# A decode step on one core: weights loaded first and the FFN run early, wo in two halves, output in eight adjacent partitions with one store, filler matmuls near the end

## Chip, cores, metric

One core of one Trainium2 chip. The metric is the device time of one launch in microseconds (us), lower is better. Most executions of one kernel agree within 0.3%, but some runs fall into a slower state. Each run is labelled fast or slow, and only fast runs are compared. A ratio is the mean time of one kernel's fast runs over the mean of the other kernel's fast runs of the same rounds, so it is not quite the ratio of the medians quoted beside it.

## The reference, cut to what matters

```python
# x: [2, 1, 448]; 16 query heads, 8 KV heads, head size 256; only the last W = 2048 cache rows count
xn = layernorm(x)
q  = xn @ wq                                  # wq: [448, 4096]
p  = softmax(q . k[:, :, -2048:] * 256**-0.5) # k_cache, v_cache: [2, 8, 8192, 256]
s  = (p . v[:, :, -2048:]) @ wo               # wo: [4096, 448]
g  = silu(relu(xn @ w1) @ w2)                 # the FFN; w1: [448, 1792], w2: [1792, 448]
out = x + s * g
```

All inputs are bf16. Two sequences, one token each: every weight and every cache row is used once or twice, so the kernel mostly moves bytes.

## The kernel before

The work is cut into four units; a unit is one sequence and four KV heads. K0 to K3 and V0 to V3 are the units' 4 MB pieces of the caches. The program gives each engine its own list of operations, and waits between engines by semaphores. PE is the matrix engine, DVE and ACT are the vector and the scalar engine, and SP issues the loads. In the FFN, H is the first matmul, hT its transpose and F the second matmul.

```python
# two K buffers, two V buffers; weights borrow them while they are free
wq_sb, w1_sb, w2_sb, wo_sb = vbuf[1], kbuf[0], kbuf[0], kbuf[1]

def do_T(u, i):       # four fp32-viewed transposes of K into a PSUM bank tb, then a copy to kt[i] by DVE or ACT
def do_S(u, g):       # scores: 8 matmuls of 512 columns in four column tiles, into sbk
def softmax(u, fill): # DVE, PE, ACT in turn; PE does "fill" (P x V of the unit before) meanwhile
def do_PV(u, gs):     # P x V, 8 matmuls for each g, four column tiles
def scores(u):        # T and S of one unit, interleaved

load_k(0); load wq; load_k(1); load_v(0)
for i in range(NCHUNK): do_T(0, i)
do_q()
for g in range(4): do_S(0, g)
load_k(2); load_v(1); softmax(0)
scores(1); load_k(3); softmax(1, values(0)); attend_scale(0); load_v(2)
scores(2)
# ... load w1, w2 into kbuf[0], free since T of unit 2
softmax(2, values(1)); attend_scale(1); load_v(3, (0, 48, 64))
scores(3)
# ... load wo in five parts into kbuf[1], free since T of unit 3
softmax(3, values(2)); attend_scale(2)
do_H(); attend_turn(2); do_hT(); do_F()          # the FFN, in the shadow of V3's load
do_PV(3); attend_scale(3); attend_turn(3)
# ... two small matmuls and copies spread the attention output to at2
for j in range(32):
    deps = deps + [landed.get(j)]
    for i in range(4):                           # four column tiles: output rows 32 i and 32 i + 1
        lo = j * D + i * NCOL                    # NCOL = 112
        m_o = pr.op(PE, mm(obk[32 * i:32 * i + B, 0:NCOL], at2[:, 2 * j:2 * j + 2], wo_sb[:, lo:lo + NCOL],
                           j == 0, j == 31, tile_position=(0, 32 * i)), deps)
# ... s * g, + x on 128 partitions, then two stores (one for each sequence) from every 32nd partition
```

Of the kernel before, what the change touches and what calls it, by code (L numbers as in the profile page):

```python
# [5 lines left out]
BF = mybir.dt.bfloat16  # L6
# [70 lines left out]
def bass_recurrent_scan__sliding_block_cached__dense_activation_relu__decode_kernel(  # L77
# [28 lines left out]
    WO_PARTS = [12, 12, 4, 2, 2]  # L106
    NCOL = D // 4
    NTB = 5
# [5 lines left out]
    with es:  # L114
# [17 lines left out]
        qmask = named("qmask", [128, 4], F32)  # L132
# [3 lines left out]
        fold = named("fold", [128, 32], BF)  # L136
        fold8 = named("fold8", [128, 8], F32)
# [11 lines left out]
        h_sb = named("h_sb", [128, 28], BF)  # L149
        x_c = named("x_c", [128, NCOL], BF)  # L150
        ea = named("ea", [128, NCOL], F32)
        g_sb = named("g_sb", [128, NCOL], F32)
        tmp = named("tmp", [128, NCOL], F32)
        out_sb = named("out_sb", [128, NCOL], BF)
# [12 lines left out]
        at_exp = named("at_exp", [128, 256], BF)  # L167
        at2 = named("at2", [128, 64], BF)
# [13 lines left out]
        def kv_src(u, cache):  # L182
# [4 lines left out]
        p_xc = pr.op(POOL, lambda e: e.memset(x_c[:, :], 0.0))  # L187
        d_xc = [pr.dma(ACTE, view(x_c, 0, [[1, NCOL]], n=4, p0=b, pstep=32),
                       A_x[b, 0, :].rearrange("(i n) -> i n", i=4), [p_xc]) for b in range(B)]

        wq_sb, w1_sb, w2_sb, wo_sb = vbuf[1], kbuf[0], kbuf[0], kbuf[1]
# [4 lines left out]
        wo_src = A_wo.rearrange("(p j) n -> p (j n)", j=32)  # L196
# [7 lines left out]
        def load_v(u, cuts=(0, NT)):  # L204
            deps = [None if u == 0 else st["q_mm"] if u == 1 else st["PV", u - 2]]
            d_v[u] = []
            for lo, hi in zip(cuts, cuts[1:]):
                d_v[u].append((hi, pr.dma(SP, vbuf[u % 2][:, lo * DH:hi * DH],
                                          kv_src(u, A_v_cache)[:, :, lo * DH:hi * DH], deps)))

        load_k(0)
        d_wq = pr.dma(SP, wq_sb[:, 0:SLOTS * HC], wq_src)
        load_k(1)
        load_v(0)
# [10 lines left out]
        p_qz = pr.op(POOL, lambda e: e.memset(qz[:, :], 0.0), [p_one])  # L225

# [9 lines left out]
        for e2 in range(2):  # L236
# [10 lines left out]
            out=qmask[:, :], in_=view(ident, 0, [[32, 4], [1, 32]]), axis=AX.X, op=ALU.add))  # L247
# [4 lines left out]
        v_fold = pr.op(DVE, fold_op)  # L252
        v_f8 = pr.op(DVE, lambda e: e.tensor_reduce(
# [103 lines left out]

        def do_PV(u, gs=range(4)):
            bank, src, p = obk, vbuf[u % 2], pt[u % 2]
            for g in gs:  # L360
                deps = [next(d for hi, d in d_v[u] if hi >= 16 * g + 16), st["pt", u], a_z, st["obk"]]
                for a in range(2):
                    for i in range(4):
                        lo = (16 * g + 4 * i + 2 * a) * DH
                        o = pr.op(PE, mm(bank[32 * i:32 * i + 16, :],
                                         p[:, 256 * a + 64 * i + 16 * g:256 * a + 64 * i + 16 * g + 16], src[:, lo:lo + 2 * DH],
                                         g == 0 and a == 0, g == 3 and a == 1, tile_position=(0, 32 * i)), deps)
                        deps = []
            st["PV", u] = o

        def attend_scale(u):
            st["osb", u] = st["obk"] = pr.op(DVE, lambda e: e.tensor_scalar(  # L372
                out=o_sb[:, :], in0=obk[:, :], scalar1=rs[:, u:u + 1], scalar2=None, op0=ALU.mult),
                [st["PV", u], st["rs", u], st.get(("oT", u - 1))])

        def attend_turn(u):
            b, v = divmod(u, 2)
            deps = [st["osb", u], v_fold, st["mbk"]]
            for dhi in range(2):
                for tp in range(2):  # L380
                    o = pr.op(PE, mm(mbk_ap(136 + 8 * dhi, 8), o_sb[:, 256 * tp + 128 * dhi:256 * tp + 128 * dhi + 128],
                                     fold[:, 8 * tp:8 * tp + 8], tp == 0, tp == 1), deps)
                    deps = []
            st["oT", u] = o
            st["at", u] = st["mbk"] = pr.op(DVE, lambda e: e.tensor_tensor(
                out=view(at_exp, 128 * b + 64 * v, [[8, 8], [4, 2], [1, 4]]),
                in0=view(mbk, 136, [[1, 8], [8, 2], [0, 4]]),
                in1=view(qmask, 0, [[0, 8], [0, 2], [1, 4]]), op=ALU.mult), [o, v_qm])
# [35 lines left out]
        def do_hT():  # L424
            hbk = tb[0][:, :].bitcast(F32).tensor
            deps = [st["h_n"], evac[NU * NCHUNK - 4]]
            for j in range(7):
                for i in range(4):
                    o = pr.op(PE, mm(view(hbk, 4 * j, [[1, 4]], n=32, p0=32 * i), view(h_n, j, [[7, 32]]),
                                     ident[:, 32 * i:32 * i + 4], j == 0, tile_position=(0, 32 * i)), deps)  # L430
                    deps = []
            st["hT"] = pr.op(DVE, lambda e: e.tensor_copy(
                view(h_sb, 0, [[2, 7], [14, 2], [1, 2]]), view(hbk, 0, [[4, 7], [2, 2], [1, 2]])), [o])

        def do_F():
            fbk = tb[1][:, :].bitcast(F32).tensor
            deps = [st["w2"], st["hT"], evac[NU * NCHUNK - 3]]
            for f in range(14):
                for i in range(4):
                    lo = W2_AT + f * D + i * NCOL  # L440
                    o = pr.op(PE, mm(view(fbk, 0, [[1, NCOL]], n=B, p0=32 * i), h_sb[:, 2 * f:2 * f + 2], w2_sb[:, lo:lo + NCOL],
                                     f == 0, f == 13, tile_position=(0, 32 * i)), deps)
                    deps = []
            f_ap = view(fbk, 0, [[1, NCOL]])
            a_e = pr.op(ACTE, lambda e: e.activation(ea[:, :], f_ap, ACT.Exp, scale=-1.0), [o])
            v_d = pr.op(DVE, lambda e: e.tensor_scalar(
                out=ea[:, :], in0=ea[:, :], scalar1=1.0, scalar2=None, op0=ALU.add), [a_e])
            v_rc = pr.op(DVE, lambda e: e.reciprocal(tmp[:, :], ea[:, :]), [v_d])
            st["g"] = pr.op(DVE, lambda e: e.tensor_tensor(
                out=g_sb[:, :], in0=f_ap, in1=tmp[:, :], op=ALU.mult), [v_rc])  # L450

        def scores(u):
            for i in range(NCHUNK):
# [3 lines left out]
                if i == 3 and u > 1:  # L457
                    attend_turn(u - 2)
            do_S(u, 3)
# [4 lines left out]
        for i in range(NCHUNK):  # L464
            do_T(0, i)
        do_q()
        for g in range(4):
            do_S(0, g)
# [9 lines left out]
        st["w1"] = pr.dma(SP, w1_sb[:, 0:W2_AT], w1_src, [st["T", 2]])  # L478
        st["w2"] = pr.dma(SP, w2_sb[:, W2_AT:W2_AT + 14 * D].rearrange("p (hf f) -> p hf f", hf=2), w2_src,
                          [st["T", 2]])  # L480
        softmax(2, values(1))
        attend_scale(1)
        load_v(3, (0, 48, 64))
        scores(3)
        d_wo = []
        j0 = 0
        for n in WO_PARTS:
            d_wo.append((j0, pr.dma(SP, wo_sb[:, j0 * D:(j0 + n) * D], wo_src[:, j0 * D:(j0 + n) * D], [st["T", 3]])))
            j0 += n
        softmax(3, values(2))  # L490
        attend_scale(2)
        do_H()
        attend_turn(2)
        do_hT()
        do_F()
        do_PV(3)
        attend_scale(3)
        attend_turn(3)
        for b in range(2):
            m_at = pr.op(PE, mm(mbk_ap(256 + 32 * b, 32), at_exp[:, 128 * b:128 * b + 128],  # L500
                                fold[:, :], True, True), [st["at", NU - 1], v_fold, st["mbk"]])
            v_at2 = st["mbk"] = pr.op(DVE, lambda e, b=b: e.tensor_copy(
                view(at2, b, [[2, 32]]), mbk_ap(256 + 32 * b, 32)), [m_at])
        deps = [v_at2, st["obk"]]
        landed = dict(d_wo)
        for j in range(32):
            deps = deps + [landed.get(j)]
            for i in range(4):
                lo = j * D + i * NCOL
                m_o = pr.op(PE, mm(obk[32 * i:32 * i + B, 0:NCOL], at2[:, 2 * j:2 * j + 2], wo_sb[:, lo:lo + NCOL],  # L510
                                   j == 0, j == 31, tile_position=(0, 32 * i)), deps)
                deps = []
        v_t = pr.op(DVE, lambda e: e.tensor_tensor(
            out=tmp[:, :], in0=obk[:, 0:NCOL], in1=g_sb[:, :], op=ALU.mult), [m_o, st["g"]])
        v_o = pr.op(DVE, lambda e: e.tensor_tensor(
            out=out_sb[:, :], in0=tmp[:, :], in1=x_c[:, :], op=ALU.add), [v_t, *d_xc])
        d_o = [pr.dma((SP, ACTE)[b], out[b, 0, :].rearrange("(i n) -> i n", i=4),
                      view(out_sb, 0, [[1, NCOL]], n=4, p0=b, pstep=32), [v_o]) for b in range(B)]
        pr.op(SP, None, d_o)
# [31 lines left out]
```

## Time and profile before

| | before |
|---|---|
| time, median of the first 3 runs | 112.66 us (112.59 to 112.87) |
| span of the profiled run, first to last instruction | 110.9 us |
| bytes moved by the load queue | 44.11 MB, busy 93.5% of the span |
| K0 landed / K3 landed | 13.1 / 71.6 us |
| last softmax begins (reduction of scores of unit 3) | 82.62 us |
| wo's matmuls begin / end | 102.38 / 107.9 us |

The transfer table on the profile page of the kernel before gives, for each queue, packets, MB and the share of 16 engines' span:

```profile
q1 hardware_dynamic: 2584, 44.11, 93.5%
```

Its windows view, cut to the steady part, has the columns: start:end and length in us, busy time of each engine with its instruction count, mean granted clock of PE (1.00 is full), mean busy share of the DMA engines, GB/s:

```profile
4.00:104.00 100.00, 71.58 (x765) 48.19 (x765) 46.52 (x105) 33.85 (x42) 0.00 (x0) 0.87 1.00 429
```

For 100 us the DMA engines have a busy share of 1.00 at 429 GB/s. PE is at 71.58 us of 100.

The chain of waits of the kernel before (start, length, what), its ends alone:

```profile
0.74 12.35 DMA kbuf<-in_A_k_cache_dram
...
46.36 25.27 DMA kbuf<-in_A_k_cache_dram
...
83.07 24.39 DMA kbuf<-in_A_wo_dram
107.46 0.04 issue
107.50 0.39 PE obk L265 x8
107.89 0.02 issue
107.91 0.28 DVE tmp L513
108.19 0.02 issue
108.22 0.27 DVE out_sb L515
```

It ends in wo's last piece, and after it only 8 matmuls, two vector operations and the store are left.

The view of who waited for whom (engine, line, what it waited for: us in total, times, longest) has PE waiting for three kinds of loads only:

```profile
PE tb L285 <- DMA kbuf<-in_A_k_cache_dram: 6.3, 2, 5.4
...
PE obk L265 <- DMA vbuf<-in_A_v_cache_dram: 3.5, 1, 3.5
...
PE obk L265 <- DMA kbuf<-in_A_wo_dram: 1.8, 2, 1.6
```

Of the 6.3 us, 5.4 are the wait for K0 and 0.9 the wait for K3. So from 13.13 us to 70.8 us PE never waits for a transfer: it works, or it waits for DVE and ACT, in the softmax above all. The last softmax begins here (timeline of the kernel before):

```profile
82.62 0.69 DVE L318 TENSOR_REDUCE rm<-sbk 128x4 f32<-128x512 f32 x1 [0.73 <-PE sbk L265]
```

PE's slack is 0.9 us at K3 and whatever lies after the last softmax: the FFN, which has time there, and 3.5 us of waiting for V3. The timeline of the tail (start, length, engine, line, operation, tensors, count, idle time before and its cause) shows this, and shows that wo's matmuls come in bursts as its parts land:

```profile
96.35 3.59 PE L265 MATMUL obk<-vbuf,pt 128*16 128x512 bf16 x32 [3.49 <-DMA vbuf<-in_A_v_cache_dram]
...
102.38 1.29 PE L265 MATMUL obk<-kbuf,at 128*2 128x112 bf16 x48 [0.29 <-DVE at L502]
...
105.29 2.01 PE L265 MATMUL obk<-kbuf,at 128*2 128x112 bf16 x72 [1.62 <-DMA kbuf<-in_A_wo_dram]
...
107.50 0.36 PE L265 MATMUL obk<-kbuf,at 128*2 128x112 bf16 x8 [0.20 <-DMA kbuf<-in_A_wo_dram]
```

### The profile page before, as it was taken

The numbers are of one execution on the slowest core, as the hardware profiler recorded it, in microseconds if no ns is written. First come the engines' busy times: TensorE is split into PE (matmuls) and PEld (weight loads), VectorE is DVE, ScalarE is ACT, GpSimd is POOL, SyncE is SP. The second block draws the span as 40 slices with busy tenths as digits, with TensorE's granted clock in tenths as the row PEclk, the third lists the DMA queues.
The fourth block names the chain that finished last, engine by engine and source line by source line (L and its number), as shares of the span: only waits on it lengthen the run. The fifth ranks groups of instructions, "written<-read, shape, count | busy, mean of one in ns | idle before, by whom it ended". The sixth has DMA issues, their size and how long they took to land.

```text
span 110.9 us, 1921 instructions
## 1 busy us (share of the span) xinstructions
PE 74.0 (67%) x845; PEld 49.7 (45%) x845; DVE 48.0 (43%) x110; ACT 35.4 (32%) x43; POOL 1.9 (2%) x11
## 2 busy tenths in 40 slices
PE   0010299995428999859999949699985464293480
PEld 0000299952127977413777513397632244022350
DVE  2182042953433356553775653477546333104001
ACT  1960036760020647602286602076820200000000
POOL 6000000000000000000000000000000000000000
PEclk9999999999995589995899995799999985555555
DMA  3988979898899889889989998998999999999920
GB/s 95 473 379 379 520 331 496 355 567 372 378 532 414 378 378 556 384 378 532 417 366 390 526 402 378 520 426 378 387 382 416 454 434 423 408 426 427 394 98 1
DMA packets 2619, 44.22 MB, mean 399 GB/s; under 512 B 306, under 2 KB 564, under 8 KB 948
## 3 DMA queue, kind: packets, MB, share of 16 engines
q1 hardware_dynamic: 2584, 44.11, 93.5%
q8 instruction: 6, 0.10, 0.3%
q10 hardware_dynamic: 28, 0.00, 0.0%
q14 instruction: 1, 0.01, 0.0%
HBM read 44.11 MB, written 0.00 MB: 398 GB/s over the span
## 4 chain that ended last, share of the span: by engine, by line
DMA 56%; PE 34%; DVE 4%; SPq 2%; issue 1%; ACT 1%
DMA kbuf<-in_A_k_cache_dram 34%; PE tb L285 25%; DMA kbuf<-in_A_wo_dram 22%; PE sbk L265 5%; PE obk L265 2%; SPq L36 2%; PE mbk L265 1%; DVE s_sb L335 1%; ACT e_sb L340 1%; DVE rm L318 1%; DVE q_n L399 1%; PE mbk L345 1%; DVE pt L350 0%; DVE qz L409 0%; PE mbk L403 0%
## 5 line engine op out<-in xcount | busy, mean ns | idle before, releaser
L285 PE MATMUL tb<-ident_f,kbuf 128*128 128x128 f32 x256 | 36.6, 306 | 6.3 <-DMA kbuf<-in_A_k_cache_dram 6.3
L285 PEld LDWEIGHTS tb<-ident_f,kbuf 128*128 128x128 f32 x256 | 33.5, 161 | 10.4 <-DMA kbuf<-in_A_k_cache_dram 6.4
L295 ACT ACTIVATE kt<-tb 128x1024 bf16<-128x1024 bf16 x28 | 27.4, 1023 | 26.2 <-PE tb L285 26.2
L293 DVE COPY kt<-tb 128x1024 bf16<-128x1024 bf16 x36 | 24.7, 690 | 21.7 <-PE tb L285 21.7
L265 PE MATMUL obk<-vbuf,pt 128*16 128x512 bf16 x128 | 13.5, 529 | 3.5 <-DMA vbuf<-in_A_v_cache_dram 3.5
L265 PE MATMUL sbk<-kt,qz 128*32 128x512 bf16 x128 | 11.0, 393 | 1.7 <-DVE kt L293 1.1
L340 ACT ACTIVATE e_sb<-s_sb 128x512 bf16<-128x512 f32 x4 | 2.5, 630 | 22.9 <-DVE s_sb L335 22.9
L265 PEld LDWEIGHTS obk<-vbuf,pt 128*16 128x16 bf16 x128 | 3.2, 101 | 8.2 <-DMA vbuf<-in_A_v_cache_dram 4.4
L265 PE MATMUL mbk<-ident,xg 2*128 2x2 bf16 x7 | 0.3, 163 | 7.4 <-DVE xg L237 7.4
L372 DVE TENSOR_SCALAR o_sb<-obk,rs 128x512 bf16<-128x512 f32 x4 | 2.9, 735 | 5.4 <-PE obk L265 5.4
L265 PEld LDWEIGHTS sbk<-kt,qz 128*32 128x32 bf16 x128 | 2.7, 94 | 5.5 <-DVE kt L293 2.1
L265 PE MATMUL obk<-kbuf,at 128*2 128x112 bf16 x128 | 3.7, 292 | 2.1 <-DMA kbuf<-in_A_wo_dram 1.8
L318 DVE TENSOR_REDUCE rm<-sbk 128x4 f32<-128x512 f32 x4 | 2.8, 691 | 4.3 <-PE sbk L265 4.3
L350 DVE COPY pt<-mbk 128x512 bf16<-128x512 bf16 x4 | 1.7, 424 | 5.6 <-PE mbk L345 5.6
L345 PE MATMUL mbk<-ident,e_sb 128*128 128x128 bf16 x16 | 2.2, 286 | 2.6 <-ACT e_sb L340 2.6
L265 PEld LDWEIGHTS obk<-kbuf,at 128*2 128x2 bf16 x128 | 2.6, 112 | 3.1 <-DMA kbuf<-in_A_wo_dram 2.6
L265 PEld LDWEIGHTS mbk<-ident,xg 2*128 2x128 bf16 x7 | 0.3, 101 | 7.4 <-DVE xg L237 7.4
L345 PEld LDWEIGHTS mbk<-ident,e_sb 128*128 128x128 bf16 x16 | 1.3, 122 | 5.0 <-ACT e_sb L340 5.0
L323 PE MATMUL mbk<-ident_f,rm 128*1 128x128 f32 x4 | 1.1, 270 | 3.4 <-DVE rm L321 3.4
L265 PE MATMUL mbk<-one_f,mall 1*128 1x1 f32 x8 | 1.6, 268 | 2.5 <-DVE mall L330 2.5
L335 DVE SCALAR_TENSOR_TENSOR s_sb<-sbk,bias,low 128x512 f32<-128x512 f32 x4 | 3.0, 751 | 0.1
L323 PEld LDWEIGHTS mbk<-ident_f,rm 128*1 128x1 f32 x4 | 0.3, 79 | 5.4 <-DVE rm L321 5.4
(68 smaller groups left out, 37.0 us busy)
## 6 DMA issues: line engine op xcount, KB each, us to landing
kbuf<-in_A_k_cache_dram SPq DMA_DIRECT2D x4, 4096.0 KB, 27.1
vbuf<-in_A_v_cache_dram SPq DMA_DIRECT2D x3, 4096.0 KB, 37.0
vbuf<-in_A_wq_dram SPq DMA_DIRECT2D x1, 3584.0 KB, 20.1
kbuf<-in_B_w_dram SPq DMA_DIRECT2D x2, 1568.0 KB, 23.6
vbuf<-in_A_v_cache_dram SPq DMA_DIRECT2D x1, 3072.0 KB, 25.8
kbuf<-in_A_wo_dram SPq DMA_DIRECT2D x2, 1344.0 KB, 22.2
vbuf<-in_A_v_cache_dram SPq DMA_DIRECT2D x1, 1024.0 KB, 27.7
kbuf<-in_A_wo_dram SPq DMA_DIRECT2D x1, 448.0 KB, 24.3
```

What stands on the lines that cost most here:

```text
L36: o = _Op(eng, lambda e: e.dma_start(dst, src), [d for d in deps if d is not None], True)
L265: return lambda e: e.matmul(out_ap, lhsT=lhsT, rhs=rhs, start=start, stop=stop, skip_group_check=True, **kw)
L285: o = pr.op(PE, lambda e, n=n, lo=lo: e.matmul(bank_f[:, n * 128:(n + 1) * 128], lhsT=src_f[:, lo:lo + 128], rhs=ident_f[:, :], start=True ...
L293: evac[n_th] = pr.op(DVE, lambda e: e.tensor_copy(dst[:, :], bank[:, :]), deps)
L295: evac[n_th] = pr.op(ACTE, lambda e: e.activation(dst[:, :], bank[:, :], ACT.Copy), deps)
L318: v = pr.op(DVE, lambda e: e.tensor_reduce(out=rm4[:, :], in_=view(sbk, 0, [[1, 4], [4, 128]]), axis=AX.X, op=ALU.max), [st["S", u]])
L323: m = st["rmT", u] = pr.op(PE, lambda e: e.matmul(mbk_ap(0, 128, 1), lhsT=rm[:, :], rhs=ident_f[:, :], start=True, stop=True, is_transpose ...
L335: v = st["shift", u] = pr.op(DVE, lambda e: e.scalar_tensor_tensor(out=view(s_sb, 0, [[4, 128], [1, 4]]), in0=view(sbk, 0, [[4, 128], [1, ...
L340: a = st["exp", u] = pr.op(ACTE, lambda e: e.activation(e_sb[:, :], s_sb[:, :], ACT.Exp, accum_out=ssum[:, 0:1]), [v, st.get(("Pt", u - 1) ...
L345: o = pr.op(PE, lambda e, j=j: e.matmul(mb16[:, 512 + 128 * j:640 + 128 * j], lhsT=e_sb[:, 128 * j:128 * j + 128], rhs=ident[:, :], start= ...
L350: v = st["pt", u] = pr.op(DVE, lambda e: e.tensor_copy(view(pt[u % 2], 0, [[256, 2], [16, 16], [8, 2], [1, 8]]), view(mb16, 512, [[256, 2] ...
L372: st["osb", u] = st["obk"] = pr.op(DVE, lambda e: e.tensor_scalar(out=o_sb[:, :], in0=obk[:, :], scalar1=rs[:, u:u + 1], scalar2=None, op0 ...
```

## The change

The intent: get the small weights and the whole FFN out of the way at the start, so that the end has less to do; let half of wo's work depend on half of the heads; shorten the end with a compact output and one store; and keep PE busy near the end so that its clock stays up.

The core of the diff (cut):

```diff
-        wq_sb, w1_sb, w2_sb, wo_sb = vbuf[1], kbuf[0], kbuf[0], kbuf[1]
+        wq_sb, w1_sb, w2_sb, wo_sb = vbuf[1], vbuf[0], vbuf[0], kbuf[0]
...
-            deps = [None if u == 0 else st["q_mm"] if u == 1 else st["PV", u - 2]]     # load_v
+            deps = [st["F"] if u == 0 else st["q_mm"] if u == 1 else st["PV", u - 2]]
...
+        d_wq = pr.dma(SP, wq_sb[:, 0:SLOTS * HC], wq_src)
+        st["w1"] = pr.dma(SP, w1_sb[:, 0:W2_AT], w1_src)
+        st["w2"] = pr.dma(SP, w2_sb[:, ...], w2_src)
         load_k(0)
-        d_wq = pr.dma(SP, wq_sb[:, 0:SLOTS * HC], wq_src)
         load_k(1)
-        load_v(0)
...
-        for i in range(NCHUNK):
-            do_T(0, i)
         do_q()
-        for g in range(4):
-            do_S(0, g)
+        do_H()
+        do_hT()
+        do_F()
+        load_v(0)
+        scores(0)
...
         attend_scale(2)
-        do_H()
-        attend_turn(2)
-        do_hT()
-        do_F()
-        do_PV(3)
+        idle_work(3)                  # 3 matmuls of 512 columns that nobody reads
+        do_PV(3, (0,))                # P x V of unit 3, now into another bank (tb[3])
+        attend_turn(2)
+        do_PV(3, (1,))
+        attend_spread(2)
+        do_PV(3, (2, 3))
         attend_scale(3)
+        idle_work(3)
         attend_turn(3)
-        for b in range(2): ...        # two spreads, one after the other
+        idle_work(1)
+        attend_spread(3)
...
-                m_o = pr.op(PE, mm(obk[32 * i:32 * i + B, 0:NCOL], at2[:, 2 * j:2 * j + 2], wo_sb[:, lo:lo + NCOL],
-                                   j == 0, j == 31, tile_position=(0, 32 * i)), deps)
+                m_o = pr.op(PE, mm(obk[0:NROW, 0:NCOL], at_z[:, j * GAP + 3 - i:j * GAP + 3 - i + NROW],
+                                   wo_sb[:, lo:lo + NCOL], j == 0 and i == 0, j == 2 * NWO - 1 and i == 3), deps)
...
-        d_o = [pr.dma((SP, ACTE)[b], ...) for b in range(B)]
+        d_o = pr.dma(ACTE, out[:, 0, :].rearrange("b (i n) -> (b i) n", i=4), out_sb[:, :], [v_o])
```

In the new layout each of the four 112-column pieces writes all eight output rows; the weights are zero except in the two columns that belong to its own piece, and a shift of the window into a zero-padded buffer selects them. The FFN's second matmul (F) has the same layout. wo's parts became 6, 6, 4, 4, 4, 4, 2, 2 slices instead of 12, 12, 4, 2, 2, and its buffer is free already after the transposes of unit 2.

More of the change, by code (lines that the diff above doesn't have):

```diff
@@ L105, in bass_recurrent_scan__sliding_block_cached__dense_activation_relu__decode_kernel @@
     FC = DFF // 2
-    WO_PARTS = [12, 12, 4, 2, 2]
+    WO_PARTS = [6, 6, 4, 4, 4, 4, 2, 2]
+    NWO = 16
     NCOL = D // 4
+    NROW = 4 * B
+    GAP = NROW + 3
     NTB = 5
@@ L131, in bass_recurrent_scan__sliding_block_cached__dense_activation_relu__decode_kernel @@
         par2 = named("par2", [128, 2], F32)
-        qmask = named("qmask", [128, 4], F32)
+        qmask = named("qmask", [128, 8], F32)
         own = named("own", [128, 4], F32)
@@ L136, in bass_recurrent_scan__sliding_block_cached__dense_activation_relu__decode_kernel @@
         fold = named("fold", [128, 32], BF)
+        fold16 = named("fold16", [128, NWO], BF)
         fold8 = named("fold8", [128, 8], F32)
@@ L148, in bass_recurrent_scan__sliding_block_cached__dense_activation_relu__decode_kernel @@
         h_n = named("h_n", [128, FC // 4], BF)
-        h_sb = named("h_sb", [128, 28], BF)
-        x_c = named("x_c", [128, NCOL], BF)
-        ea = named("ea", [128, NCOL], F32)
-        g_sb = named("g_sb", [128, NCOL], F32)
-        tmp = named("tmp", [128, NCOL], F32)
-        out_sb = named("out_sb", [128, NCOL], BF)
+        h_z = named("h_z", [128, 14 * GAP], BF)
+        x_c = named("x_c", [NROW, NCOL], BF)
+        ea = named("ea", [NROW, NCOL], F32)
+        g_sb = named("g_sb", [NROW, NCOL], F32)
+        tmp = named("tmp", [NROW, NCOL], F32)
+        out_sb = named("out_sb", [NROW, NCOL], BF)
         rm4 = named("rm4", [128, 4], F32)
@@ L166, in bass_recurrent_scan__sliding_block_cached__dense_activation_relu__decode_kernel @@
         o_sb = named("o_sb", [128, 512], BF)
-        at_exp = named("at_exp", [128, 256], BF)
-        at2 = named("at2", [128, 64], BF)
+        at_exp = named("at_exp", [128, 128], BF)
+        at_z = named("at_z", [128, 32 * GAP], BF)
         kbuf = [named(f"kbuf{i}", [128, UW], BF) for i in range(2)]
@@ L186, in bass_recurrent_scan__sliding_block_cached__dense_activation_relu__decode_kernel @@
         d_x = pr.dma(ACTE, x_sb[0:B, :], A_x[:, 0, :])
-        p_xc = pr.op(POOL, lambda e: e.memset(x_c[:, :], 0.0))
-        d_xc = [pr.dma(ACTE, view(x_c, 0, [[1, NCOL]], n=4, p0=b, pstep=32),
-                       A_x[b, 0, :].rearrange("(i n) -> i n", i=4), [p_xc]) for b in range(B)]
-        wq_sb, w1_sb, w2_sb, wo_sb = vbuf[1], kbuf[0], kbuf[0], kbuf[1]
+        d_xc = pr.dma(ACTE, x_c[:, :], A_x[:, 0, :].rearrange("b (i n) -> (b i) n", i=4))
+        wq_sb, w1_sb, w2_sb, wo_sb = vbuf[1], vbuf[0], vbuf[0], kbuf[0]
         W2_AT = SLOTS * FC
@@ L195, in bass_recurrent_scan__sliding_block_cached__dense_activation_relu__decode_kernel @@
         w2_src = B_w2.rearrange("(hf p j) n -> p hf (j n)", hf=2, j=7)
-        wo_src = A_wo.rearrange("(p j) n -> p (j n)", j=32)
+        wo_src = A_wo.rearrange("(v p j) n -> v p (j n)", v=2, j=NWO)
         assert SLOTS * HC <= UW and 32 * D <= UW and W2_AT + 14 * D <= UW
@@ L209, in load_v @@
                                           kv_src(u, A_v_cache)[:, :, lo * DH:hi * DH], deps)))
+        d_wq = pr.dma(SP, wq_sb[:, 0:SLOTS * HC], wq_src)
+        st["w1"] = pr.dma(SP, w1_sb[:, 0:W2_AT], w1_src)
+        st["w2"] = pr.dma(SP, w2_sb[:, W2_AT:W2_AT + 14 * D].rearrange("p (hf f) -> p hf f", hf=2), w2_src)
         load_k(0)
-        d_wq = pr.dma(SP, wq_sb[:, 0:SLOTS * HC], wq_src)
         load_k(1)
-        load_v(0)
         i0 = pr.op(POOL, lambda e: e.memset(ident[:, :], 0.0))
@@ L225, in bass_recurrent_scan__sliding_block_cached__dense_activation_relu__decode_kernel @@
         p_qz = pr.op(POOL, lambda e: e.memset(qz[:, :], 0.0), [p_one])
+        p_z = [pr.op(POOL, lambda e, t=t: e.memset(t[:, :], 0.0)) for t in (h_z, at_z)][-1]
         a_z = [pr.op(ACTE, lambda e, t=t: e.memzero(t[:, :])) for t in (obk,)][-1]
@@ L246, in bass_recurrent_scan__sliding_block_cached__dense_activation_relu__decode_kernel @@
         v_qm = pr.op(DVE, lambda e: e.tensor_reduce(
-            out=qmask[:, :], in_=view(ident, 0, [[32, 4], [1, 32]]), axis=AX.X, op=ALU.add))
+            out=qmask[:, :], in_=view(ident, 0, [[16, 8], [1, 16]]), axis=AX.X, op=ALU.add))
         def fold_op(e):
@@ L252, in bass_recurrent_scan__sliding_block_cached__dense_activation_relu__decode_kernel, with fold16_op @@
         v_fold = pr.op(DVE, fold_op)
+        def fold16_op(e):
+            with nc.allow_low_precision("zeros and ones"):
+                return e.tensor_reduce(out=fold16[:, :], in_=view(ident, 0, [[1, NWO], [NWO, 8]]), axis=AX.X, op=ALU.add)
+        v_fold16 = pr.op(DVE, fold16_op)
         v_f8 = pr.op(DVE, lambda e: e.tensor_reduce(
@@ L356, in softmax, with out_bank @@
             assert not fill
+        obk_last = tb[3][:, :].bitcast(F32).tensor
+        def out_bank(u):
+            return obk if u < NU - 1 else obk_last
         def do_PV(u, gs=range(4)):
-            bank, src, p = obk, vbuf[u % 2], pt[u % 2]
+            bank, src, p = out_bank(u), vbuf[u % 2], pt[u % 2]
             for g in gs:
-                deps = [next(d for hi, d in d_v[u] if hi >= 16 * g + 16), st["pt", u], a_z, st["obk"]]
+                deps = [next(d for hi, d in d_v[u] if hi >= 16 * g + 16), st["pt", u], a_z if u < NU - 1 else st["tb3"], st["obk"]]
                 for a in range(2):
@@ L371, in attend_scale @@
         def attend_scale(u):
-            st["osb", u] = st["obk"] = pr.op(DVE, lambda e: e.tensor_scalar(
-                out=o_sb[:, :], in0=obk[:, :], scalar1=rs[:, u:u + 1], scalar2=None, op0=ALU.mult),
+            v = st["osb", u] = pr.op(DVE, lambda e: e.tensor_scalar(
+                out=o_sb[:, :], in0=view(out_bank(u), 0, [[1, 512]]), scalar1=rs[:, u:u + 1], scalar2=None, op0=ALU.mult),
                 [st["PV", u], st["rs", u], st.get(("oT", u - 1))])
+            if u < NU - 1:
+                st["obk"] = v
         def attend_turn(u):
-            b, v = divmod(u, 2)
             deps = [st["osb", u], v_fold, st["mbk"]]
@@ L385, in attend_turn, with attend_spread @@
             st["at", u] = st["mbk"] = pr.op(DVE, lambda e: e.tensor_tensor(
-                out=view(at_exp, 128 * b + 64 * v, [[8, 8], [4, 2], [1, 4]]),
-                in0=view(mbk, 136, [[1, 8], [8, 2], [0, 4]]),
-                in1=view(qmask, 0, [[0, 8], [0, 2], [1, 4]]), op=ALU.mult), [o, v_qm])
+                out=view(at_exp, 0, [[16, 8], [8, 2], [1, 8]]),
+                in0=view(mbk, 136, [[1, 8], [8, 2], [0, 8]]),
+                in1=view(qmask, 0, [[0, 8], [0, 2], [1, 8]]), op=ALU.mult), [o, v_qm, st.get(("m_at", u - 1))])
+        def attend_spread(u):
+            b, v = divmod(u, 2)
+            o = st["m_at", u] = pr.op(PE, mm(mbk_ap(256, NWO), at_exp[:, :], fold16[:, :], True, True),
+                                      [st["at", u], v_fold16, st["mbk"]])
+            st["at_z", v] = st["mbk"] = pr.op(DVE, lambda e: e.tensor_copy(
+                view(at_z, NWO * GAP * v + 3 + 4 * b, [[GAP, NWO]]), mbk_ap(256, NWO)), [o, p_z])
         def do_q():
@@ L425, in do_hT @@
             hbk = tb[0][:, :].bitcast(F32).tensor
-            deps = [st["h_n"], evac[NU * NCHUNK - 4]]
+            deps = [st["h_n"]]
             for j in range(7):
@@ L431, in do_hT @@
                     deps = []
-            st["hT"] = pr.op(DVE, lambda e: e.tensor_copy(
-                view(h_sb, 0, [[2, 7], [14, 2], [1, 2]]), view(hbk, 0, [[4, 7], [2, 2], [1, 2]])), [o])
+            st["hT"] = evac[-NTB] = pr.op(DVE, lambda e: e.tensor_copy(
+                view(h_z, 3, [[GAP, 7], [7 * GAP, 2], [4, 2]]), view(hbk, 0, [[4, 7], [2, 2], [1, 2]])), [o, p_z])
         def do_F():
             fbk = tb[1][:, :].bitcast(F32).tensor
-            deps = [st["w2"], st["hT"], evac[NU * NCHUNK - 3]]
+            deps = [st["w2"], st["hT"]]
             for f in range(14):
@@ L440, in do_F @@
                     lo = W2_AT + f * D + i * NCOL
-                    o = pr.op(PE, mm(view(fbk, 0, [[1, NCOL]], n=B, p0=32 * i), h_sb[:, 2 * f:2 * f + 2], w2_sb[:, lo:lo + NCOL],
-                                     f == 0, f == 13, tile_position=(0, 32 * i)), deps)
+                    o = pr.op(PE, mm(view(fbk, 0, [[1, NCOL]], n=NROW), h_z[:, f * GAP + 3 - i:f * GAP + 3 - i + NROW],
+                                     w2_sb[:, lo:lo + NCOL], f == 0 and i == 0, f == 13 and i == 3), deps)
                     deps = []
-            f_ap = view(fbk, 0, [[1, NCOL]])
+            st["F"] = o
+            f_ap = view(fbk, 0, [[1, NCOL]], n=NROW)
             a_e = pr.op(ACTE, lambda e: e.activation(ea[:, :], f_ap, ACT.Exp, scale=-1.0), [o])
@@ L448, in do_F, with idle_work @@
             v_rc = pr.op(DVE, lambda e: e.reciprocal(tmp[:, :], ea[:, :]), [v_d])
-            st["g"] = pr.op(DVE, lambda e: e.tensor_tensor(
+            st["g"] = evac[1 - NTB] = pr.op(DVE, lambda e: e.tensor_tensor(
                 out=g_sb[:, :], in0=f_ap, in1=tmp[:, :], op=ALU.mult), [v_rc])
+        def idle_work(n):
+            wbk = tb[2][:, :].bitcast(F32).tensor
+            deps = [evac[NU * NCHUNK - 2], v_fold]
+            for _ in range(n):
+                pr.op(PE, mm(view(wbk, 0, [[1, 512]]), ident[:, :], kt[0][:, 0:512], True, True), deps)
+                deps = []
         def scores(u):
@@ L458, in scores @@
                     attend_turn(u - 2)
+                if i == 5 and u > 1:
+                    attend_spread(u - 2)
             do_S(u, 3)
@@ L477, in bass_recurrent_scan__sliding_block_cached__dense_activation_relu__decode_kernel @@
         scores(2)
-        st["w1"] = pr.dma(SP, w1_sb[:, 0:W2_AT], w1_src, [st["T", 2]])
-        st["w2"] = pr.dma(SP, w2_sb[:, W2_AT:W2_AT + 14 * D].rearrange("p (hf f) -> p hf f", hf=2), w2_src,
-                          [st["T", 2]])
         softmax(2, values(1))
@@ L483, in bass_recurrent_scan__sliding_block_cached__dense_activation_relu__decode_kernel @@
         load_v(3, (0, 48, 64))
-        scores(3)
-        d_wo = []
-        j0 = 0
-        for n in WO_PARTS:
-            d_wo.append((j0, pr.dma(SP, wo_sb[:, j0 * D:(j0 + n) * D], wo_src[:, j0 * D:(j0 + n) * D], [st["T", 3]])))
-            j0 += n
+        d_wo, j0 = {}, 0
+        for n in WO_PARTS:
+            v, j = divmod(j0, NWO)
+            d_wo[j0] = pr.dma(SP, wo_sb[:, j0 * D:(j0 + n) * D], wo_src[v, :, j * D:(j + n) * D], [st["T", 2]])
+            j0 += n
+        scores(3)
+        st["tb3"] = pr.op(ACTE, lambda e: e.memzero(tb[3][:, :]), [evac[NU * NCHUNK - 1]])
@@ L490, in bass_recurrent_scan__sliding_block_cached__dense_activation_relu__decode_kernel @@
         softmax(3, values(2))
         attend_scale(2)
-        do_H()
+        idle_work(3)
+        do_PV(3, (0,))
         attend_turn(2)
-        do_hT()
-        do_F()
-        do_PV(3)
+        do_PV(3, (1,))
+        attend_spread(2)
+        do_PV(3, (2, 3))
         attend_scale(3)
+        idle_work(3)
         attend_turn(3)
-        for b in range(2):
-            m_at = pr.op(PE, mm(mbk_ap(256 + 32 * b, 32), at_exp[:, 128 * b:128 * b + 128],
-                                fold[:, :], True, True), [st["at", NU - 1], v_fold, st["mbk"]])
-            v_at2 = st["mbk"] = pr.op(DVE, lambda e, b=b: e.tensor_copy(
-                view(at2, b, [[2, 32]]), mbk_ap(256 + 32 * b, 32)), [m_at])
@@ L504, in bass_recurrent_scan__sliding_block_cached__dense_activation_relu__decode_kernel @@
-        deps = [v_at2, st["obk"]]
-        landed = dict(d_wo)
-        for j in range(32):
-            deps = deps + [landed.get(j)]
+        idle_work(1)
+        attend_spread(3)
+        deps = [st["obk"]]
+        for j in range(2 * NWO):
+            deps = deps + [d_wo.get(j), st["at_z", j // NWO]]
             for i in range(4):
                 lo = j * D + i * NCOL
-                m_o = pr.op(PE, mm(obk[32 * i:32 * i + B, 0:NCOL], at2[:, 2 * j:2 * j + 2], wo_sb[:, lo:lo + NCOL],
-                                   j == 0, j == 31, tile_position=(0, 32 * i)), deps)
+                m_o = pr.op(PE, mm(obk[0:NROW, 0:NCOL], at_z[:, j * GAP + 3 - i:j * GAP + 3 - i + NROW],
+                                   wo_sb[:, lo:lo + NCOL], j == 0 and i == 0, j == 2 * NWO - 1 and i == 3), deps)
@@ L512, in bass_recurrent_scan__sliding_block_cached__dense_activation_relu__decode_kernel @@
                 deps = []
         v_t = pr.op(DVE, lambda e: e.tensor_tensor(
-            out=tmp[:, :], in0=obk[:, 0:NCOL], in1=g_sb[:, :], op=ALU.mult), [m_o, st["g"]])
+            out=tmp[:, :], in0=obk[0:NROW, 0:NCOL], in1=g_sb[:, :], op=ALU.mult), [m_o, st["g"]])
         v_o = pr.op(DVE, lambda e: e.tensor_tensor(
-            out=out_sb[:, :], in0=tmp[:, :], in1=x_c[:, :], op=ALU.add), [v_t, *d_xc])
-        d_o = [pr.dma((SP, ACTE)[b], out[b, 0, :].rearrange("(i n) -> i n", i=4),
-                      view(out_sb, 0, [[1, NCOL]], n=4, p0=b, pstep=32), [v_o]) for b in range(B)]
@@ L519, in bass_recurrent_scan__sliding_block_cached__dense_activation_relu__decode_kernel @@
-        pr.op(SP, None, d_o)
+            out=out_sb[:, :], in0=tmp[:, :], in1=x_c[:, :], op=ALU.add), [v_t, d_xc])
+        d_o = pr.dma(ACTE, out[:, 0, :].rearrange("b (i n) -> (b i) n", i=4), out_sb[:, :], [v_o])
+        pr.op(ACTE, None, [d_o])
         with nc.Block() as block:
```

## The prediction

> **What bounds it now.** The page's transfer table: 44.11 MB, SP's queue busy 93.5% of the 110.9 us span. Windows show about 427 GB/s from 2.4 us on, with no gap, and the chain of waits ends in wo's last piece (landed 107.46), then 8 matmuls (0.39), two vector operations (0.6) and the store (2.4). Bytes do not change; the tail leaves at most about 1 us to win.
>
> **PE is nearly as tight.** The timeline shows no DMA wait on PE between K0's landing (13.13) and 70.8 us, where K3 comes 0.9 us late. The slack is in the last stage: H, hT and F (89.1 to 92.9) and a 3.5 us wait for V3 before 96.35.
>
> **What the change moves.** Landings of before fit 3.15 us + cumulative bytes / 0.4215 MB per us (K0 13.1, wq 21.5, K3 71.6, end 107.5). With wq, w1, w2 ahead, K0 lands at about 29.4 instead of 13.1. Moved out of its path: q (3.4 us) and H/hT/F, which were free in the slack. From there the serial work per unit, from the timeline (scores to score maximum, then softmax to the next transpose): 13.2+5.9, 13.2+6.1, 10.8+6.1, 10.9+5.5 = 71.7 us. The two 13.2 include a slow clock at their start (28 transposes in 5.68 us; at full clock 16 take 1.90). So softmax 3 ends near 101 us (before: 88.1), after V3 has landed (about 99). I see no new DMA starvation: V0 waits for F (about 25 us, queue full to 39), K2, V1, K3, V2, V3 are all issued before the queue drains. wo still lands near 107.5, but no longer matters.
>
> **Tail after 101.** Fillers, PV3 with turn and spread of unit 2 (about 3 us), scale 0.75, turn, spread (about 1.2): wo's matmuls start near 106 (before: 102.4). Before, four column tiles ran together: 56 such matmuls of 112 columns took 1.47 us at half clock, 26 ns each. Now the eight adjacent rows put all in one column group, so they run one after another: 4 x 26 = about 105 ns cold, about 50 warm (bf16 transposes of 128 columns step about 50 ns at full clock: four in 0.40 us). The Trainium skill ("TensorE: Matmul & The Clock Gate", Part 3 and "Back-to-back issue gap") agrees: tiles overlap by column group; alone N/2.4+2.5 ns, and 81 ns for load/matmul pairs at N=128. 128 of them: estimate 6.4 us warm, 10 at the pair rate, 13 cold; I take 7. End of wo about 113, plus 3.0 us for combine and store: span 116, timed 117.8.
>
> Single store, no memset, 8-partition vector work: under 0.3 us together. Smaller wo pieces: nothing. Fillers: about 1.5 us of PE, partly hidden behind the scale; they hold the clock up for wo.
>
> **Prediction: 117.8 us, range 114.9 to 121.5. Faster 2%, same 13%, slower 85%.**
>
> **Right if** the profile shows K0's landing near 29 us; PE waiting for no transfer after that; softmax 3 ending near 101; wo's matmuls one stream of 6 to 10 us starting near 106, with all wo landed before they finish; the chain of waits running through PE and DVE from K0 to the end instead of ending in a wo transfer.
>
> **Wrong if** the clock is granted earlier than before in the first two score stages (up to 2.4 us each) and wo runs warm: then the wo transfer bounds again and the time is about 112.5. Or worse, if weight loads are exposed or the clock stays at 0.5 in the tail: 121 and more. Or if transfers starve somewhere in the middle.

## The result, and the profile after

| | before | after |
|---|---|---|
| time, median | 112.71 us (112.59 to 112.87, 4 runs) | 119.18 us (117.83 to 120.74, 4 runs) |
| fast runs | all 4 | 117.91 and 117.83 |
| ratio of fast runs | | 1.0457, 95% interval 1.0432 to 1.0482 |
| span of the profiled run | 110.9 us | 116.1 us (fast) |
| K0 landed | 13.1 us | 30.25 us |
| last softmax begins | 82.62 us | 96.19 us |
| wo's matmuls begin / end | 102.38 / 107.9 us | 107.4 / 113.9 us |

The change is slower by 4.6%. Two of its four runs fell at 120.5 and 120.7 us, which is why its median lies so far above the fast runs; the fast runs alone are used below.

The transfers hardly got slower. The transfer table on the profile page of the kernel after:

```profile
q1 hardware_dynamic: 3008, 44.11, 90.0%
```

Its windows view over the same stretch as before:

```profile
4.00:104.00 100.00, 74.19 (x690) 49.17 (x692) 45.77 (x104) 33.56 (x42) 0.00 (x0) 0.86 1.00 424
```

The busy share is 1.00 again, at 424 GB/s, and of the page's 40 slices each from the second to the 36th has the DMA engines at 80% or more: no stretch is starved. The chain of waits of the kernel after, however, is another one:

```profile
2.11 28.14 DMA kbuf<-in_A_k_cache_dram
30.25 0.04 issue
30.29 5.00 PE tb L294 x28
...
107.48 6.40 PE obk L274 x128
...
113.91 0.27 DVE tmp L542
...
114.20 0.26 DVE out_sb L544
```

The first reduction of the last softmax (timeline of the kernel after) comes 13.6 us later than before:

```profile
96.19 0.69 DVE L327 TENSOR_REDUCE rm<-sbk 128x4 f32<-128x512 f32 x1 [0.73 <-PE sbk L274]
```

After K0's landing at 30.25 us no DMA stands in the chain any more; from there to the end it runs through PE, DVE and ACT, and its last large piece is one unbroken stretch of 128 matmuls. In the view of who waited for whom, for the kernel after, PE's waits for loads are now all in the first 31 us:

```profile
PE tb L294 <- DMA kbuf<-in_A_k_cache_dram: 5.8, 1, 5.8
...
PE obk L274 <- DMA vbuf<-in_A_wq_dram: 5.2, 1, 5.2
...
PE tb L274 <- DMA vbuf<-in_B_w_dram: 0.6, 1, 0.6
```

PE waits for loads only until K0 has landed; after that no load holds it up. The tail in the timeline of the kernel after, beside that of before:

```profile
102.45 0.59 PE L274 MATMUL tb<-kt,ident 128*128 128x512 bf16 x2
...
102.49 0.73 DVE L386 TENSOR_SCALAR o_sb<-obk,rs 128x512 bf16<-128x512 f32 x1
...
103.37 0.61 PE L274 MATMUL tb<-vbuf,pt 128*16 128x512 bf16 x8 [0.33 <-DVE o_sb L386]
...
105.72 0.82 PE L274 MATMUL tb<-kt,ident 128*128 128x512 bf16 x3
105.85 0.75 DVE L386 TENSOR_SCALAR o_sb<-tb,rs 128x512 bf16<-128x512 f32 x1 [0.75 <-PE tb L274]
...
106.66 0.26 PE L274 MATMUL mbk<-fold,o_sb 128*128 128x8 bf16 x4
...
107.41 6.46 PE L274 MATMUL obk<-kbuf,at_z 128*8 128x112 bf16 x128
```

The last line is wo: the 128 matmuls that before came in bursts, at 27 to 28 ns each (2.01 us for 72, granted clock 0.50), with waits for transfers between them, now take 6.40 us in one piece, 50 ns each, and wait for nothing. The windows view of the kernel after, cut to this stretch, shows that its clock is full and that the transfers are over:

```profile
107.40:114.00 6.60, 6.47 (x129) 6.29 (x128) 0.32 (x2) 0.00 (x0) 0.00 (x0) 1.00 0.01 3
```

The fillers (the lines `tb<-kt,ident`) run while DVE does its two scale operations. The first line shows two of the three: a few matmul records are missing from a trace. The first P x V of unit 3 still waits 0.33 us for the first scale operation after the fillers before it are done.

### The profile page after: what moved, and what is told of

Read it like the earlier page. It is cut to its first block, busy times and chain, and to the rows that moved or that the text cites. A ratio compares the mean times of both kernels' runs of the same rounds, so it can differ in the third digit from the quotient of the medians.

```text
span 116.1 us, 1945 instructions
## 1 busy us (share of the span) xinstructions
PE 83.8 (72%) x853; PEld 56.5 (49%) x854; DVE 49.0 (42%) x113; ACT 35.9 (31%) x44; POOL 2.3 (2%) x12
## 4 chain that ended last, share of the span: by engine, by line
PE 56%; DMA 24%; DVE 13%; ACT 2%; issue 2%; SPq 1%
PE tb L294 30%; DMA kbuf<-in_A_k_cache_dram 24%; PE obk L274 10%; PE sbk L274 8%; PE mbk L274 4%; DVE kt L302 2%; DVE rm L327 2%; PE mbk L354 2%; DVE s_sb L344 2%; ACT e_sb L349 2%; PE tb L274 2%; DVE o_sb L386 1%; SPq L36 1%; DVE mrow L335 1%; PE mbk L332 1%
## 5 line engine op out<-in xcount | busy, mean ns | idle before, releaser
L294 PEld LDWEIGHTS tb<-ident_f,kbuf 128*128 128x128 f32 x256 | 32.4, 158 | 11.3 <-DMA kbuf<-in_A_k_cache_dram 6.0
L302 DVE COPY kt<-tb 128x1024 bf16<-128x1024 bf16 x36 | 24.8, 691 | 21.6 <-PE tb L294 21.1
L274 PE MATMUL sbk<-kt,qz 128*32 128x512 bf16 x128 | 12.0, 394 | 1.5 <-DVE kt L302 1.5
L274 PE MATMUL obk<-vbuf,pt 128*16 128x512 bf16 x96 | 11.0, 550 | 0.0
L274 PE MATMUL obk<-vbuf,xr 128*4 128x512 bf16 (+1 forms) x56 | 4.6, 506 | 5.2 <-DMA vbuf<-in_A_wq_dram 5.2
L274 PE MATMUL obk<-kbuf,at_z 128*8 128x112 bf16 x128 | 6.5, 213 | 0.0
L274 PEld LDWEIGHTS obk<-kbuf,at_z 128*8 128x8 bf16 x128 | 6.3, 87 | 0.0
L274 PE MATMUL tb<-vbuf,h_z 128*8 128x112 bf16 x56 | 4.7, 275 | 0.6 <-DMA vbuf<-in_B_w_dram 0.6
L274 PEld LDWEIGHTS obk<-vbuf,xr 128*4 128x4 bf16 x56 | 1.6, 115 | 7.2 <-DMA vbuf<-in_A_wq_dram 5.3
L274 PEld LDWEIGHTS tb<-vbuf,h_z 128*8 128x8 bf16 x56 | 4.6, 118 | 0.7 <-DMA vbuf<-in_B_w_dram 0.7
L274 PEld LDWEIGHTS obk<-vbuf,pt 128*16 128x16 bf16 x96 | 2.4, 100 | 2.8 <-issue 1.9
```

The costliest lines, as they stand in the source:

```text
L274: return lambda e: e.matmul(out_ap, lhsT=lhsT, rhs=rhs, start=start, stop=stop, skip_group_check=True, **kw)
L294: o = pr.op(PE, lambda e, n=n, lo=lo: e.matmul(bank_f[:, n * 128:(n + 1) * 128], lhsT=src_f[:, lo:lo + 128], rhs=ident_f[:, :], start=True ...
L302: evac[n_th] = pr.op(DVE, lambda e: e.tensor_copy(dst[:, :], bank[:, :]), deps)
```

## Experiments

Two causes were in the prediction: K0 lands late, so that PE's serial work moves past the end of the transfers (theory A), and wo's matmuls lost their packing (theory B). Rivals: one of the two alone is the whole loss; the fillers are on the path; or the transfers are starved. The last is already answered by the busy share above. All eight kernels gave correct results.

### e1_order_only: the load order and the early FFN alone

```diff
 # on the kernel before
+        load wq; load w1; load w2            # w1, w2 into vbuf[0]; V0 waits for F
         load_k(0)
-        load wq
         load_k(1)
-        load_v(0)
...
-        T(0); q; S(0)
+        do_q(); do_H(); do_hT(); do_F(); load_v(0); scores(0)
...                                            # wo into kbuf[0], after T of unit 2
-        do_H(); attend_turn(2); do_hT(); do_F(); do_PV(3)
+        attend_turn(2); do_PV(3)
```

> Before, with only the new load order (wq, w1, w2, K0, K1, V0 after F), FFN first, and wo behind V3 in the buffer that K2 frees; four column tiles, layouts and store as before. My theory (K0 late makes the PE chain of about 72 us the bound): K0 lands near 30, softmax 3 ends near 102, wo's matmuls start at 107 to 109 and take 2 to 3.5 us as four tiles: 115.0 to 117.0 us, no PE wait for a wo transfer. Rival (the serial wo stream is what costs, the order alone is harmless): 112 to 113.5 us. Second rival (the whole loss is the order, the layout costs nothing): 117.5 to 118.5.

Measured: 115.28 us median (114.17 to 117.37, 4 runs, one of them slow); ratio 1.0183 (1.0128 to 1.0237). The verdict at 2% is "unclear", but the interval excludes no loss. In the timeline of e1:

```profile
96.77 0.69 DVE L319 TENSOR_REDUCE rm<-sbk 128x4 f32<-128x512 f32 x1 [0.73 <-PE sbk L266]
...
108.36 2.11 PE L266 MATMUL obk<-kbuf,at 128*2 128x112 bf16 x128 [0.29 <-DVE at L499]
```

The last softmax begins at 96.77 us, as late as in the kernel after, and wo's 128 matmuls wait for no part of wo. So the order alone moves the bound to PE, and costs about 2 us (fast runs 114.91 us on average, against 112.85 for before). Part of the 2.11 us is a falling clock: windows of e1 show it at 1.00 up to 109.2 us and at 0.50 from 109.6 us, 0.79 on average over the stream. It is not the whole loss, and it is not harmless: two of the three expectations are excluded.

### e2_wo_tiled: the eight-row layout alone undone

```diff
 # on the kernel after (F likewise; combine on 128 rows and two stores as before)
-   mm(obk[0:NROW, 0:NCOL], at_z[:, j * GAP + 3 - i:j * GAP + 3 - i + NROW], wo_sb[...], ...)
+   mm(obk[32 * i:32 * i + B, 0:NCOL], view(at_z, j * GAP + 3, [[4, B]]), wo_sb[...], ..., tile_position=(0, 32 * i))
```

> After, with only the eight adjacent rows undone: FFN's second and wo's matmuls again in four column tiles, 128-row combine, two stores. My theory: wo takes 2 to 3.4 us where it took 6.4, the store 0.8 more: 114.5 to 116 us in the faster state, still slower than before by 2 to 3%, since K0 still lands near 30. Rival (the serial stream is the whole loss): about 112.7. Rival (packing does not matter here, the stream is bound by something else): 118 to 119.

Measured: 114.29 us (114.0 to 116.73, 4 runs, one slow); ratio to before 1.0127 (1.0103 to 1.0151). wo's matmuls in the timeline of e2:

```profile
107.35 1.75 PE L276 MATMUL obk<-kbuf,at_z 128*2 128x112 bf16 x128
```

The windows view of e2, cut to that stretch:

```profile
107.40:109.20 1.80, 1.69 (x129) 1.52 (x128) 0.28 (x2) 0.00 (x0) 0.00 (x0) 1.00 0.04 13
```

The stream starts at the same time as in the kernel after (107.35 against 107.41 us) at the same full clock, and takes 1.70 us by the chain of waits instead of 6.40: 13 ns a matmul instead of 50. I had expected 2 to 3.4 us. The 3.4 is 128 times the 26 ns that the kernel before showed at half clock; halved for the full clock that is 1.7, and my lower end of 2 did not go that far. Four tiles at full clock ran here at about a quarter of the serial time. Of the 4.7 us won the strided stores take back about 0.8 (below), and the ratio of the two ratios, 1.0457 / 1.0127, is 3.3% or 3.7 us. The remainder, 1.3% or 1.4 us, is what the new order costs here, with the two halves and the fillers still in place; in e1, without them, it cost 2.1. The packing alone is not the whole loss either.

### e3_no_fill: the kernel after without the fillers

```diff
-        idle_work(3)    # before P x V of unit 3
-        idle_work(3)    # during the scale of unit 3
-        idle_work(1)    # before the spread of unit 3
```

> After, without the seven filler matmuls. My theory: they sit in PE's waits for the two scale operations, so taking them away saves at most 0.3 us by itself; the clock may drop in the tail, and then the serial wo stream starts at half clock (50 ns becomes 95 ns each until it is granted again): 117.8 to 121. Rival (the fillers are a cost on the path): 116.5 to 117.2.

Measured: 118.46 us (117.86 to 120.54, 4 runs, one slow); ratio 1.0479 (1.0440 to 1.0519), not to be told from the 1.0457 of the kernel after. wo's matmuls in the timeline of e3:

```profile
108.22 6.46 PE L274 MATMUL obk<-kbuf,at_z 128*8 128x112 bf16 x128
```

The windows view of e3, cut to that stretch:

```profile
108.00:115.00 7.00, 6.57 (x129) 6.38 (x129) 0.54 (x3) 0.00 (x0) 0.00 (x0) 1.00 0.02 5
```

The stream takes the same 6.46 us and the clock is full without the fillers. From the start of the last softmax to the start of wo it took 11.25 us here (96.97 to 108.22) and 11.22 with the fillers (96.19 to 107.41). In this kernel the fillers cost nothing measurable, as they sit in PE's waits for the scale operations, and gain nothing, as the clock was full without them. My prediction had given them a use that they do not have here. Whether they have one for packed matmuls is open: in e1, packed and without fillers, the clock fell inside wo's stream (2.13 us by its chain of waits), in e2, packed and with fillers, it did not (1.70), but the two differ in other parts too, and no run separates them.

### e4_old_order: the kernel after with only the order undone

```diff
 # on the kernel after: loads, buffers and FFN's place as in the kernel before
-        load wq; load w1; load w2; load_k(0); load_k(1)
+        load_k(0); load wq; load_k(1); load_v(0)
...
-        do_q(); do_H(); do_hT(); do_F(); load_v(0); scores(0)
+        T(0); q; S(0)
...                                  # w1, w2 loaded behind K3, wo after T of unit 3
         attend_scale(2)
+        do_H(); do_hT(); do_F()
         idle_work(3)
```

> After, with only the load order and FFN's place undone (K0, wq, K1, V0 first, w1 and w2 behind K3, wo in the buffer that K3 frees; FFN before PV3), eight-row layout, two halves, one store and fillers kept. My theory: K0 lands near 13, DMA bounds again, wo lands near 107.5, V3 near 99, wo's matmuls start near 101.5 to 102.5 and, if the clock is full, keep up with the transfers: 112.0 to 113.5 us. If the clock is half in the tail the serial stream needs 12 us and the time is 115 to 118. Rival (serial stream and fillers are the whole loss): 116 to 119 with wo ending 6 us after its start.

Measured: 113.09 us (112.73 to 113.53, 4 runs, all fast); ratio 1.0023 (0.9988 to 1.0058). With K0 first again, all other parts of the change together are worth nothing measurable. The timeline of its tail (e4):

```profile
102.22 6.46 PE L273 MATMUL obk<-kbuf,at_z 128*8 128x112 bf16 x128
...
109.30 0.30 ACTq L36 DMA_DIRECT2D out_dram<-out_sb  x1
```

The chain of waits of e4 ends in no transfer of wo; it runs from K3's landing through PE:

```profile
45.23 26.43 DMA kbuf<-in_A_k_cache_dram
...
102.29 6.40 PE obk L273 x128
```

The same serial stream of 6.4 us starts 5.2 us earlier than in the kernel after, so most of it runs while wo is still arriving (DMA share 0.87 from 105 to 106 us, 0.43 in the next, 0.09 after that). It ends at 108.7 us, 0.8 later than the matmuls of before, and the compact store gives that back: from the store's issue to the end of the span it takes 1.6 us (109.30 to 110.9), as in the kernel after (114.50 to 116.1), where the two strided stores of before take 2.4 (108.52 to 110.9). Shown here: the serial layout costs its 4.7 us in full only when the transfers are over before the stream starts; in e4 the stream comes last too, but ends only 0.8 us later than the packed one of before. The two causes are not a sum. The order alone cost 2.1 us (e1) and the rest alone 0.3 (e4); together they cost 5.1.

### e5_before_wq_first: a smaller dose of the delay

```diff
 # on the kernel before
-        load_k(0)
-        load wq
+        load wq
+        load_k(0)
         load_k(1)
...
-        T(0); q; S(0)
+        do_q(); scores(0)
```

> Before, with wq loaded ahead of K0 and nothing else moved (q runs before the first transposes): a smaller dose of the same delay, K0 near 20.5 instead of 13. My theory (a delay of K0 costs only what exceeds the slack that PE had, about 8 us, and q leaves its path): softmax 3 ends near 92 to 94, before V3 lands, so no loss: 111.8 to 113.0 us. Rival (every microsecond of K0's delay shows in the end): 115 to 119.

Measured: 112.79 us (112.59 to 114.54, 5 runs, one slow); ratio 0.9988 (0.9976 to 1.0001). Its last softmax begins 4.4 us later than before (timeline of e5), and the chain of waits of e5 still ends in wo's transfer:

```profile
87.05 0.69 DVE L318 TENSOR_REDUCE rm<-sbk 128x4 f32<-128x512 f32 x1 [0.73 <-PE sbk L265]
...
87.43 20.22 DMA kbuf<-in_A_wo_dram
...
107.69 0.39 PE obk L265 x8
```

A delay of 4.4 us in PE's work is free, one of 13.6 (96.19 less 82.62) is not: the delay first uses up slack, as theory A says.

### e9_wq_behind_k0: the change with one load moved

```diff
 # on the kernel after
-        load wq; load w1; load w2; load_k(0); load_k(1)
+        load w1; load w2; load_k(0); load wq; load_k(1)
...
-        do_q(); do_H(); do_hT(); do_F(); load_v(0); scores(0)
+        do_H(); do_hT(); do_F(); load_v(0); T(0); q; S(0)
```

> After, with one load moved: wq behind K0 (w1, w2, K0, wq, K1), so that FFN still runs first but K0 lands near 20.5; q runs after the transposes of unit 0. My theory: PE's chain ends about 8 to 9 us earlier than in after, softmax 3 near 94 to 96, V3 bounds again, and only the serial wo stream is left: 112.3 to 113.8 us. If the clock is half when wo starts: 115 to 117. Rival (FFN first or the serial layout is what costs, not when K0 lands): 117 to 119.

Measured: 113.88 us (112.59 to 114.65, 6 runs, two slow); ratio of the fast runs 1.0033 (0.9991 to 1.0075). Its profiled run is a slow one, so I take from it only when K0 landed, which happens before PE has any part in the chain (chain of waits of e9):

```profile
1.64 20.00 DMA kbuf<-in_A_k_cache_dram
...
21.68 9.66 PE tb L294 x64
```

With 3.67 MB fewer ahead of K0 it lands at 21.6 us, and 4.2 of the 4.6% are gone, with FFN still first, the serial wo, the fillers and the single store in place. This is the sharpest test of theory A: it keeps the early FFN, which a rival might have blamed. One more thing moves with the load: q needs wq, and so runs after the transposes of unit 0 instead of ahead of them, which makes PE's chain longer and not shorter.

### e7_old_order_early_wo and e10_wq_behind_k0_early_wo: can the parts be put together to win?

```diff
 # on e4_old_order, and on e9_wq_behind_k0
         attend_scale(3)
-        idle_work(3)
+        do_wo(range(6))               # wo's first 6 slices, which need no result of unit 3
         attend_turn(3); idle_work(1); attend_spread(3)
-        wo, all 32 slices
+        do_wo(range(6, 32))
```

> The old-order kernel of the first set (eight rows, one store), with the first 6 of wo's 32 slices multiplied while DVE scales unit 3 instead of three fillers. There the serial stream of 128 matmuls ran from 102.2 to 108.7 without a wait, 0.8 us beyond before's. My theory: the stream, not wo's transfer, ends the chain there, so starting 24 matmuls early ends it near 107.9, and with the shorter store the time is 111.8 to 112.4, under before. Rival (the transfer ends the chain already): no change, 112.7 to 113.3.

> The same, with wo's first 6 slices multiplied during the scale of unit 3. Expected 0.5 to 0.9 us under the kernel without it: 111.6 to 113.0 us.

Measured: e7 112.60 us (112.38 to 114.02, 6 runs), ratio 1.0010 (0.9970 to 1.0051); e10 112.96 us (112.83 to 113.57, 6 runs), ratio 1.0019 (1.0000 to 1.0038). Neither beats the kernel before. The profiled run of e7 is at the slow end of its runs (114.02) and shows one reason: F, now serial too, ran almost wholly at half clock there (granted clock 0.54 on average; timeline of e7),

```profile
94.67 5.07 PE L273 MATMUL tb<-kbuf,h_z 128*8 128x112 bf16 x56 [0.45 <-DVE h_z L453]
```

5.07 us where the packed F of before took 1.47 at half clock, and held back P x V of unit 3 until 100.42 us. In e10 the chain ends in a transfer again, and 32 serial matmuls follow it (chain of waits of e10):

```profile
82.78 24.22 DMA kbuf<-in_A_wo_dram
...
107.04 1.75 PE obk L274 x32
```

1.75 us after the wait where before had 0.39 with 8 packed ones. The difference, 1.36 us, is more than the 0.8 us that the compact store saves. The last softmax of e10 begins at 90.47 us, 7.9 later than before, and yet its time is 0.4% above that of before at most: with this somewhat different tail, 7.9 us of delay cost next to nothing. Both expectations were a little too hopeful (I had hoped for a time under that of before in e7, and 0.5 to 0.9 us between e9 and e10; the fast runs differ by 0.15 us, inside the spread). I did not run a version with packed matmuls and a compact store: the compact rows are what forces the single column group, and an extra step that gathers four tiles into eight rows would have to cost less than 0.8 us. Whether it can is open.

## Why the prediction was right

The fast runs came to 117.9 us, and 117.8 was predicted. The path was right, but an agreement to 0.1 us is partly luck: wo's start was predicted 1.4 us too early, its stream 0.5 too long (7 against 6.46), and the end after it 0.8 too long (3.0 against 2.2), and these errors cancel.

- **What bounds the kernel before.** Right: the transfers, with 0.9 us of slack for PE up to the last stage and the rest behind the last softmax. e5 shows that 4.4 us of delay are free; e1 (14.2 us) and the kernel after (13.6) show that delays of that size are not.
- **K0's landing.** Predicted 29.4 us from a straight line through the landings of before, measured 30.25.
- **PE's serial chain.** Predicted 71.7 us from K0's landing to the end of the last softmax, read off the timeline of before in pieces. Measured 72.1 (30.29 to the start of unit 3's reciprocal at 102.41). It worked because that chain contains no wait for a transfer: it could be moved as a block.
- **wo's start.** Predicted near 106, measured 107.4. Of the missing 1.4 us K0 is 0.9 and the chain 0.4.
- **Packing.** Right in kind and in size: 50 ns each at full clock, predicted about 50; 6.4 us for the stream, predicted 6.4 warm (I had taken 7). e2, with the same start and the same clock, shows that the packing makes the difference. The estimate for pairs of weight load and matmul from the Trainium skill, "TensorE: Matmul & The Clock Gate", "Back-to-back issue gap", 81 ns at N = 128, did not apply; its N/2.4 + 2.5 ns, which is 49 ns at 112 columns, did.
- **The end.** Store and layout were predicted to give less than 0.3 us. The mis-sized term is the store: it saves 0.8 us (2.4 to 1.6 from issue to the end of the span).
- **Fillers.** Wrong in their use: I wrote that they "hold the clock up for wo". e3 shows the same clock and the same 6.46 us without them. They cost nothing either, where I had put 1.5 us of PE, partly hidden.
- **Not foreseen.** That the two causes are not a sum: order alone 2.1 us, the rest alone 0.3, together 5.1. The prediction costed only the whole.

The slow runs of several kernels, 2 to 3 us above their fast ones, are not explained here.

## What to carry to other kernels

A chain that contains no wait for a transfer is a block that starts when its first input lands: before moving loads ahead of that input, add the block's length to the new landing time and compare it with the time at which the loads end. Averages (PE busy 67%, DMA 94%) do not show this; the list of waits for transfers, with their times, does. Giving up the packing of small matmuls cost nothing measurable where most of the stream ran while its data was still arriving (e4), and the full factor, 3.8 here, where the stream came after the last transfer; what is left to do after the last transfer counts in between (1.75 us against 0.39 in e10). So judge a layout together with what it will be waiting for.

## What the Trainium skill lacked or had wrong

- "TensorE: Matmul & The Clock Gate", "Back-to-back issue gap": the figure of about 81 ns for a sustained pair of weight load and matmul at N = 128 was not seen. 128 pairs with 8 weight columns and N = 112 ran at 50 ns each (6.40 us), close to the page's figure for an isolated gap (49 ns at N = 112); the weight loads cost nothing visible. The page does not say how wide its weights were, so this shows only that the figure does not carry over to weights of 8 columns.
- The same page, "Part 3: Packing small matmuls", gives a 2.38-fold gain for three column tiles at N = 512. It has no measured figure for four column tiles, nor for small N: here four tiles of 2 columns at N = 112 gained 3.8-fold (6.40 us to 1.70), 13 ns a matmul. Its "Wait — 56ns, not 53.3ns?" says that the time from start to start is never below about 25 ns; across column tiles it was, on average, though Part 3 of the page itself draws tiles that start about 4 ns apart.
- The same page, "Part 4: PE-mode transpose", says that full clock does not engage for transposes. In the kernel after PE had issued nothing but transposes (viewed as fp32) since 48.8 us when the granted clock went from 0.50 (window 53.5 to 54.0) to 1.00 (window 54.6 to 55.0); in the kernel before, with nothing but such transposes since 34.4 us, it did the same between 39.5 and 40.2 us.
- "DMA: Bandwidth & Descriptors", "Where 436 GB/s comes from", says without a condition that for transfers between HBM and SBUF the limit of about 358 GB/s binds. With one core running, 429 GB/s were held for 100 us, close to the page's 435 for the fabric. The skill is right elsewhere, a few lines above on the same page: there 358 is the share when both cores of a pair stream.
- No page says what a small store costs by its shape: eight rows of 224 bytes took 1.6 us from issue to the end of the span as one store from adjacent partitions, 2.4 us as two stores of four rows from every 32nd partition.
